# Means of the two directly multiplied tiles by two halving adds each, idle products gathered around them, and the opening's order dealt anew

## Chip, core and metric

One core of one Trainium2 chip. The metric is the device time of one execution in microseconds; 413.33 us is the median of three runs before the change (413.1 to 413.67).

## What is computed

Input x is 2048 tokens of 512 numbers. Cut to what matters:

```
x  = A_x                                   # 1 x 2048 x 512
xn = layernorm(x)
s  = attention(xn, wqkv) @ wo              # 32 heads of 16, each position looks at 8 positions, 2 apart
g  = silu(gelu(layernorm(xn) @ w1 + b1) @ w2 + b2)   # hidden width 1376
return x + s * g
```

The two layer norms each take a mean over the 512 numbers of a token and subtract it.

## The kernel before

Tokens are split by parity into two classes (an attention window of step 2 never leaves its class), each of 8 tiles of 128 tokens. The attention goes by units of one class and one block of eight heads (8 units, u = 0 to 7). A unit's q, k and v come from `qkv` (products at L864: per tile three groups of four products, the high half of x by the high half of wqkv, low by high, high by low, since numbers are kept as a high and a low fp16 half). VectorE does the attention itself (L930, L933, L988 ...). The hidden layer (L1143, L1186), interleaved with it on TensorE, and the output products (L1056, L1088) fill the rest of the program.

The change lies in the opening, before the first tile of unit 0. There:

- SyncE's queue loads, in this kernel's words: `t` 6 and 7 (in_A_xt_dram, 256 KB each: tiles 6 and 7 of class 0 already transposed, into U), `x` 0 to 7 (in_A_x_dram, 256 KB each, into prod), `q` 0 and 2 (the two halves of wqkv block 0, 384 KB each, into prod), `q` 4 and 6 (the halves of block 1, into U), and pieces of w1 and b1 (in_B_w_dram, in_B_b_dram).
- Tiles 6 and 7 are "direct": `center` sums the four 128-row blocks of the transposed tile to one (tile 6: a VectorE reduction at L685, then one fp32 product with a matrix of 1/512 at L691; tile 7: four fp32 products at L682) and VectorE subtracts the mean that these leave in PSUM (L693). `direct` then multiplies the centred fp32 tile by the unscaled fp32 wqkv block (L700: four products a tile). The trace has two records for one fp32 product of L682, L691 and L700.
- The other tiles: statistics on VectorE (L659, L660), factors (L714 to L731), scaling by ScalarE (L742, L744), VectorE (L751) or GpSimd (L748), then either four transposing products (L766) with high and low halves written by ScalarE (L770) and VectorE (L772, L773), or a transposing DMA (L756 to L758).
- The scale of a wqkv block comes from its squares: ScalarE squares each half with a running sum (L597), two small products with the matrix `fours` add over the partitions (L513), five VectorE instructions make a power of two (L524 to L542), and then ScalarE writes the high halves (L619) and VectorE (L626) or GpSimd (L553, L554) the low ones.
- `WAKE` idle products (L1305, `fours` by a 256-column bf16 operand, into a PSUM bank that nothing reads) can stand anywhere on TensorE's queue; 24 of them do, some between the others' work up to 56 us.

Every step is an operation with a number, counted as it is added to the plan, and the table `ORDER` (L73) lists all 1269 numbers in the order in which they are issued; an engine runs its own in that order and waits for what an operation reads. `MEANBY` says for each direct tile who sums.

Of the kernel before, what the change touches and what calls it, by code (L numbers as in the profile page):

```python
# [13 lines left out]
ALU = mybir.AluOpType  # L14
# [53 lines left out]
MEANBY = ('dve', 'pe', 'pool', 'pool')  # L68
# [299 lines left out]
PU1 = 0.969  # L368
PWARM = 0.9
PEV = 0.2698  # L370

PTOT = 0.5899

WAKE = 24
PS1 = 1.1561

QHI = 4

PQLO = 0.5225

# [19 lines left out]
def tile_mixer(ctx, tc, a_x, a_xt, a_wqkv, a_wo, b_w1, b_b1, b_w2, out):  # L400
    nc = tc.nc
    pl = Plan()
# [270 lines left out]
    def center(i):  # L673
        n = FP.index(i)
# [852 lines left out]
```

## Time and profile before

| | us |
|---|---|
| median of three runs | 413.33 (413.1 to 413.67) |
| the profiled execution | 412.45 |
| its span, first to last instruction | 410.6 |
| TensorE busy | 403.6 (98%), granted clock 1.000 |
| VectorE busy | 381.7 (93%) |
| ScalarE busy | 225.3 (55%) |
| GpSimd busy | 132.8 (32%) |

The profiled execution is 1.85 us longer than its span. Chain and timeline rows begin with the start and the duration in us from the span's first instruction; `L` numbers are lines of the program before; where the time is in square brackets it is idle time of the engine before the row, with what ended it. The records overlap on TensorE (a product's record lasts longer than the distance to the next), so the chain's rows, which do not overlap, are used for sums.

### The profile page before, as it was taken

What the parts mean: (1) busy time and instruction counts of PE and PEld (TensorE: products, weight loads), DVE (VectorE), ACT (ScalarE), POOL (GpSimd) and SP (SyncE); (2) the same over time, 40 slices, a digit from 0 to 9 for tenths busy, and PEclk for the clock granted to TensorE, in tenths of its full rate; (3) what the DMA queues carried; (4) which work ended last, traced back from release to release, by engine and by line L of the source; (5) the groups of instructions that cost most, each with busy time, mean ns of one, the idle gap of its engine ahead of it and who ended that gap; (6) DMA issues with size and microseconds to landing.
All of it is one profiled execution on the core that took longest, in us unless ns stands there. A gap on an engine that the chain in (4) does not pass through costs nothing.

```text
span 410.6 us, 5500 instructions
## 1 busy us (share of the span) xinstructions
PE 403.6 (98%) x2035; PEld 199.3 (49%) x2035; DVE 381.7 (93%) x386; ACT 225.3 (55%) x372; POOL 132.8 (32%) x141
## 2 busy tenths in 40 slices
PE   7999999999999999999999999999999999999996
PEld 4665544444444455445544554444445544444443
DVE  4999999999999999999889999899999989989985
ACT  4899987983989736633564164114523177236310
POOL 3833000053552434243423344233322505250012
PEclk9999999999999999999999999999999999999999
DMA  8947437240018372911251008610244462004874
GB/s 300 388 105 233 165 110 199 89 180 26 1 30 197 77 130 79 165 32 27 51 145 23 0 2 215 208 51 25 104 120 122 107 137 59 0 1 117 271 209 180
DMA packets 52627, 48.04 MB, mean 117 GB/s; under 512 B 37066, under 2 KB 37510, under 8 KB 52088
## 3 DMA queue, kind: packets, MB, share of 16 engines
q1 hardware_dynamic: 52600, 47.69, 41.8%
q8 instruction: 16, 0.26, 0.3%
q14 instruction: 11, 0.09, 0.1%
HBM read 24.40 MB, written 7.34 MB: 77 GB/s over the span
## 4 chain that ended last, share of the span: by engine, by line
PE 97%; DVE 1%; DMA 1%; ACT 0%; issue 0%; ACTq 0%; DVEq 0%
PE ps L864 30%; PE ps L1143 25%; PE z L1186 25%; PE ps L1056 5%; PE z L1088 2%; PE ps L1088 2%; PE z L1174 2%; PE pl L864 1%; PE pl L700 1%; DMA U<-in_A_xt_dram 1%; PE pl L1088 1%; PE z L700 1%; PE z L1177 1%; PE z L766 1%; PE z L1305 0%; DVE U L1120 0%
## 5 line engine op out<-in xcount | busy, mean ns | idle before, releaser
L864 PE MATMUL ps<-wq,yT 128*128 128x384 f16 (+1 forms) x708 | 129.3, 337 | 0.1
L1186 PE MATMUL z<-w,h 128*128 128x512 f16 x480 | 111.4, 379 | 0.0
L1143 PE MATMUL ps<-yT,w 128*128 128x512 f16 x480 | 109.1, 379 | 0.0
L864 PEld LDWEIGHTS <-yT 128*128 128x128 f16 x744 | 72.3, 98 | 58.5 <-issue 1.1
L930 DVE TENSOR_TENSOR prod<-U 128x2048 f32<-128x2048 f32 x32 | 73.8, 2312 | 4.1 <-ACT U L882 3.0
L1143 PEld LDWEIGHTS <-w 128*128 128x128 f16 x480 | 46.7, 98 | 55.6 <-issue 0.5
L933 DVE TENSOR_REDUCE L<-prod 128x128 f32<-128x2048 f32 x32 | 73.0, 2282 | 0.5
L1186 PEld LDWEIGHTS <-h 128*128 128x128 f16 x480 | 46.5, 98 | 54.6 <-issue 0.7
L999 POOL TENSOR_TENSOR prod<-prod,prod 128x1024 f32<-128x1024 f32 x14 | 41.3, 2970 | 81.4 <-DVE prod L988 81.4
L882 ACT ACTIVATE U<-ps,cs 128x384 f32<-128x384 f32 x54 | 30.2, 577 | 62.9 <-PE ps L864 62.7
L988 DVE TENSOR_TENSOR prod<-pl,U 128x2048 f32<-128x2048 f32 x28 | 63.5, 2283 | 0.3
L1156 ACT ACTIVATE ps<-ps,b1T,hsc 128x512 f32<-128x512 f32 x40 | 29.9, 748 | 37.2 <-PE ps L1143 37.0
L1159 ACT ACTIVATE h<-ps,hsc 128x512 f16<-128x512 f32 x40 | 27.4, 685 | 20.5 <-PE z L1186 19.5
L1009 POOL COPY gate<-prod 1x1 f32<-1x1 f32 x21 | 4.6, 221 | 102.2 <-DVE prod L930 102.2
L1010 POOL TENSOR_TENSOR prod<-prod 128x1024 f32<-128x1024 f32 x14 | 32.8, 2346 | 0.0
L1161 DVE SCALAR_TENSOR_TENSOR h<-ps,hsc,h 128x512 f16<-128x512 f32 x40 | 29.5, 744 | 3.3 <-ACT h L1159 3.3
L1056 PE MATMUL ps<-wo,oT 128*128 128x512 f16 x96 | 21.5, 379 | 0.0
L983 DVE TENSOR_TENSOR prod<-prod,prod 128x2048 f32<-128x2048 f32 x9 | 20.6, 2288 | 0.2
L971 ACT ACTIVATE o<-prod,osc 128x1024 f16<-128x1024 f32 (+1 forms) x9 | 9.5, 1052 | 18.1 <-DVE prod L983 9.9
L1010 POOL TENSOR_TENSOR prod<-prod,prod 128x1024 f32<-128x1024 f32 x7 | 16.4, 2347 | 0.0
L1088 PEld LDWEIGHTS <-oT 128*128 128x128 f16 x108 | 10.5, 98 | 10.4 <-issue 0.2
L1056 PEld LDWEIGHTS <-oT 128*128 128x128 f16 x96 | 9.4, 98 | 11.1
(201 smaller groups left out, 397.2 us busy)
## 6 DMA issues: line engine op xcount, KB each, us to landing
f<-in_A_x_dram SPq DMA_DIRECT2D x31, 256.0 KB, 3.1
U<-U SPq DMA_DIRECT2D x16, 392.0 KB, 6.2
gd<-f SPq DMA_DIRECT2D x12, 256.0 KB, 4.3
prod<-in_A_x_dram SPq DMA_DIRECT2D x8, 256.0 KB, 6.2
oT<-in_B_w_dram SPq DMA_DIRECT2D x2, 1024.0 KB
yT<-in_B_w_dram SPq DMA_DIRECT2D x2, 1024.0 KB
f<-gd SPq DMA_DIRECT2D x8, 256.0 KB, 5.0
out_dram<-f SPq DMA_DIRECT2D x8, 256.0 KB
```

The source lines that it names most:

```text
L864: nc.tensor.matmul(b.t[:, 0:wide], y[:, s, k, o:o + P], wq[hb][:, t, k], start=(n == 0), stop=(n == 11))
L882: act(384, lambda i=i, b=b: nc.scalar.activation(U3[:, i:i + 31:15, :], b.t[:, 0:384].rearrange("p (t e) -> p t e", t=3), AF.Identity, sca ...
L930: dve(2048, lambda p2=p2, g=g: nc.vector.tensor_tensor(p2(), q, slots(Ut, KH, 2 * g), op=ALU.mult), qk + [("kh", ub, 0), ("kh", ub, 1), (" ...
L933: dve(2048, lambda pr=pr, g=g: nc.vector.tensor_reduce(L3()[:, 2 * g:2 * g + 2], pr.t.rearrange("p (r f d) -> p r f d", r=2, d=DH), AX.X, ...
L988: dve(2048, lambda: nc.vector.tensor_tensor(pr.t.rearrange("p (r f d) -> p r f d", r=2, d=DH), A3()[:, 2 * g:2 * g + 2].rearrange("p r (f ...
L999: pool(2.4, lambda n=n: nc.gpsimd.tensor_tensor(acc.t[:, n:n + 1024], acc.t[:, n:n + 1024], p1.t[:, n:n + 1024], op=ALU.add), [acc, p1], [ ...
L1010: nc.gpsimd.tensor_tensor(x.t[:, 0:1024], x.t[:, 0:1024], y(), op=ALU.add)
L1056: nc.tensor.matmul(b.t, oT[:, hb, i // 4, s, i % 4], wo[:, t, hb], start=(hb == 0 and n == 0), stop=(hb == last and n == 2))
L1088: nc.tensor.matmul(b.t[:, cols], oT[:, hb, i // 4, s, i % 4], wo[:, t, hb, cols], start=(start and hb == 0 and n == 0), stop=(stop and hb ...
L1143: nc.tensor.matmul(b.t[0:M], w1[:, s, f * 512 + k * M:f * 512 + (k + 1) * M], yT[ch][:, t, k], start=(n == 0), stop=(n == 11))
L1156: act(512, lambda: nc.scalar.activation(b.t[0:M], b.t[0:M], AF.Gelu_apprx_tanh, bias=b1T[0:M, f:f + 1], scale=hsc[0:M, 1:2]), [b, ("b1T",) ...
L1186: nc.tensor.matmul(z.t, hl[s][:, t * P:(t + 1) * P], w2[:, w, f], start=(f == 0 and n == 0), stop=False)
```

## The change

- `MEANBY` becomes `halves` for both direct tiles: VectorE adds the upper two 128-row blocks to the lower two (128x256) and then the halves of the result (128x128), and one fp32 product follows, for tile 6 and tile 7 alike.
- `WAKE` goes from 24 to 23 idle products.
- `ORDER` is a new permutation, from the first entry to the last. Since tile 7 has one operation more and there is one idle product less, the total stays 1269.

```
-MEANBY = ('dve', 'pe', 'pool', 'pool')
+MEANBY = ('halves', 'halves', 'pool', 'pool')
...
-    0, 1, 240, 19, 2, 3, 4, 5, 6, 7, 8, 9, 10, 11, 133, 129, 113, 120, 112, 115, 130, 20, 21, 32, 33, 168, 114,
...
+    3, 0, 6, 4, 1, 2, 5, 7, 55, 19, 26, 33, 34, 111, 112, 113, 114, 115, 116, 117, 118, 119, 120, 121, 122, 123,
+    124, 125, 126, 127, 128, 20, 129, 27, 38, 28, 21, 168, 130, 131, 132, 133, 35, 36, 39, 8, 10, 9, 15, 11, 16,
...
-WAKE = 24
+WAKE = 23
...
         elif MEANBY[n] == "dve":
             dve(512, lambda: nc.vector.tensor_reduce(f3()[:, 0], x3.rearrange("p k t -> p t k"), AX.X, ALU.add),
                 [("xt", i)], [f], port=False, c=0.45)
+        elif MEANBY[n] == "halves":
+            with pl.fuse():
+                dve(256, lambda: nc.vector.tensor_tensor(f3(), x3[:, 0:2], x3[:, 2:4], op=ALU.add), [("xt", i)], [f])
+                dve(128, lambda: nc.vector.tensor_tensor(f3()[:, 0], f3()[:, 0], f3()[:, 1], op=ALU.add), [f], [f])
```

Lines behind L686 move down by four in the changed program (L691 becomes L695, L700 L704, L766 L770, L1305 L1309 and so on).

SyncE's queue, the first loads before (the operands name the tensors; in_A_xt is `t`, in_A_x `x`, in_A_wqkv `q`):

```order
L1258 DMA U_94<-in_A_xt_dram 128x512
L588 DMA prod_100<-in_A_wqkv_dram 128x768 x2
L1233 DMA prod_101<-in_A_x_dram 128x512 x2
L588 DMA U_94<-in_A_wqkv_dram 128x768
L1258 DMA U_94<-in_A_xt_dram 128x512
```

and in the changed program:

```order
L1237 DMA prod_100<-in_A_x_dram 128x512
L1262 DMA U_94<-in_A_xt_dram 128x512 x2
L1237 DMA prod_100<-in_A_x_dram 128x512
L588 DMA prod_101<-in_A_wqkv_dram 128x768 x2
L588 DMA U_94<-in_A_wqkv_dram 128x768
```

The halves of wqkv block 0 move from the second and third place behind both transposed tiles and two x tiles (tiles 2 and 0), to the fifth and sixth; tile 7's transposed load moves from the seventh place to the third. The sixth load before and the seventh in the changed program is the first half of block 1.

TensorE's queue from the mean of tile 6 to the first transposition before (`first` holds the matrix of 1/512 and the identity, `pl` and z_148 the direct tiles 6 and 7, s_126 the sums of squares of wqkv block 0 and s_127 those of block 1):

```order
L691 MATMUL ps_143<-f_103,first 128x128
L1305 MATMUL z_147<-first,fours 128x256
L700 MATMUL pl_146<-prod_100,U_94 128x384 x2
L513 MATMUL z_147<-s_126,fours 128x1
L700 MATMUL pl_146<-prod_100,U_94 128x384
L682 MATMUL ps_144<-U_94,first 128x128 x4
L700 MATMUL pl_146<-prod_100,U_94 128x384
L513 MATMUL ps_145<-s_127,fours 128x1
L766 MATMUL z_150<-first,prod_101 128x128 x4
```

and from there to the same place in the changed program (s_125 block 0, s_126 block 1):

```order
L695 MATMUL ps_143<-f_103,first 128x128
L1309 MATMUL z_147<-first,fours 128x256
L695 MATMUL ps_144<-f_104,first 128x128
L513 MATMUL z_147<-s_125,fours 128x1
L704 MATMUL pl_146<-prod_101,U_94 128x384 x3
L704 MATMUL z_148<-prod_101,U_94 128x384
L770 MATMUL z_150<-first,prod_100 128x128 x4
L513 MATMUL ps_145<-s_126,fours 128x1
L704 MATMUL pl_146<-prod_101,U_94 128x384
```

Weight loads and rows that only repeat are left out in both. Before, 7 idle products stand ahead of the mean of tile 6, 3 behind it, 1 behind the first two direct products, and 13 later. In the changed program 18 stand ahead of it, 1 between the two means, 4 behind the second, and none later; both sums of block 0 stand ahead of the first direct product, and the four products of L682 are gone.

ScalarE's queue from the high halves of block 0 on, before (L597 squares the second half of block 1, L742 and L744 scale an x tile):

```order
L619 ACTIVATE wq_82<-prod_100,qsc 128x384 x4
L770 CAST yT_89<-z_150 128x4x128
L597 ACTIVATE wq_83,s_127<-U_94 128x768
L742 ACTIVATE rb_155<-pb_154,rb_155 128x1
L744 ACTIVATE prod_101<-prod_101,rb_155 128x512
L770 CAST yT_89<-z_150 128x4x128
```

and in the changed program:

```order
L619 ACTIVATE wq_82<-prod_101,qsc 128x384 x4
L774 CAST yT_89<-z_150 128x4x128
L746 ACTIVATE rb_155<-pb_154,rb_155 128x1
L748 ACTIVATE prod_100<-prod_100,rb_155 128x512
L597 ACTIVATE wq_83,s_126<-U_94 128x768
L504 ACTIVATE wq_84,s_129<-h_113 128x4x96
L774 CAST yT_89<-z_147 128x4x128
```

The square of block 1's second half has moved behind the scaling of a tile. From there on the order of all engines differs in many places, with the same operations of the same sizes.

121 rows, old and new, of the table ORDER are left out of this document.

## The prediction

> **What bounds the kernel now.** I read the page's busy times and the head of its chain first, then the chain in order of time, since it shows where the opening ends and the steady flow begins.
>
> ```profile
> PE 403.6 (98%) x2035; PEld 199.3 (49%) x2035; DVE 381.7 (93%) x386; ACT 225.3 (55%) x372; POOL 132.8 (32%) x141
> ...
> PE 97%; DVE 1%; DMA 1%; ACT 0%; issue 0%; ACTq 0%; DVEq 0%
> ```
>
> TensorE is 97% of the chain that ends last, and VectorE is busy 93% of the span. So a microsecond counts where TensorE has no work, works slowly or does work that can be left out, and a lead of TensorE holds only if VectorE, nearly full as well, leads with it. The chain's opening rows:
>
> ```profile
> 0.74 2.70 DMA U<-in_A_xt_dram
> 3.44 0.02 issue
> 3.46 1.03 DVE f L685
> 4.49 0.04 issue
> 4.54 0.81 PE ps L691 x2
> 5.35 0.02 issue
> 5.37 0.70 DVE U L693
> 6.07 0.04 issue
> 6.11 2.93 PE pl L700 x4
> 9.04 0.21 PE z L1305
> 9.25 0.03 PE z L513 x2
> 9.29 0.78 PE pl L700 x2
> 10.06 0.89 PE ps L682 x8
> ...
> 12.06 0.44 PE z L766 x4
> 12.50 2.58 PE z L700 x8
> ...
> 15.89 0.65 PE ps L864 x4
> ...
> 27.64 1.95 PE pl L864 x12
> 29.59 0.01 PE z L518
> 29.59 1.32 PE ps L864 x8
> ...
> 40.83 0.11 PE z L1305
> ```
>
> Three things are to be seen. Up to 6.11 the chain is a load, a mean and a subtraction. The first four records of L700 take 2.93 / 4 = 0.73 us each, the eight at 12.50 2.58 / 8 = 0.32: at first TensorE runs at half rate, although the page shows a granted clock of 1.000. The row at 9.29 (two records in 0.78) has the turn. Against 0.32 each, the four cost 2.93 - 1.29 = 1.64 us. From about 24 us on the rows follow each other almost without gaps (27.64 to 29.59).
>
> **Where the loads land.** From the timeline I take who waited for a load, and when SyncE issues again: from the ninth load on an issue starts just as the load eight places before has landed (9.18 for tile 7's transposed load, 9.86 for the x tile behind it).
>
> ```profile
> 1.19 1.65 PE L1305 MATMUL z<-first,fours 128*128 128x256 bf16 x7 [1.19 <-DVE first L440]
> 4.50 0.84 ACT L597 ACTIVATE wq<-prod 128x768 bf16<-128x768 f32 x1 [2.49 <-DMA prod<-in_A_wqkv_dram]
> 5.55 0.84 ACT L597 ACTIVATE wq<-prod 128x768 bf16<-128x768 f32 x1
> 6.30 0.19 ACT L597 ACTIVATION_READ_ACCUMULATOR wq<-prod 128x1 f32 x1
> 6.35 0.69 DVE L659 BATCH_NORM_STATS2 bn<-prod 128x6 f32<-128x512 f32 x1 [0.29 <-DMA prod<-in_A_x_dram]
> 7.55 0.69 DVE L659 BATCH_NORM_STATS2 bn<-prod 128x6 f32<-128x512 f32 x1 [0.29 <-DMA prod<-in_A_x_dram]
> 8.50 0.84 ACT L597 ACTIVATE wq<-U 128x768 bf16<-128x768 f32 x1 [2.02 <-DMA U<-in_A_wqkv_dram]
> 9.18 0.33 SPq L1233 DMA_DIRECT2D prod<-in_A_x_dram  x1
> 9.86 0.33 SPq L1260 DMA_DIRECT2D h<-in_B_w_dram  x1
> ```
>
> Adding sizes in the order of issue, 256 KB are in by 3.46, 640 by 4.50, 1024 by 5.55, 1280 by 6.35, 1536 by 7.55, 1920 by 8.50, 2176 by 9.18 and 2432 by 9.86. I take it that the changed order lands the same bytes at the same times. Then an x tile is in by 3.46, the transposed tile 6 (512 KB) by 4.1, tile 7 (768) by 4.8, the next x tile (1024) by 5.55, the halves of wqkv block 0 (1408, 1792) by about 6.95 and 8.2 instead of 4.50 and 5.55; block 1's first half (2176) by 9.18 instead of 8.50, and the next x tile (2432) by 9.86, as before.
>
> **The change, part by part.** The halving adds (L689, L690) have no row of their own. The nearest are the same addition at other widths, at the end of the program and with the mean subtracted:
>
> ```profile
> 406.35 0.69 DVE L1127 TENSOR_TENSOR U<-U,f 128x512 f32<-128x512 f32 x1
> 407.47 0.42 DVE L1127 TENSOR_TENSOR U<-U 128x256 f32<-128x256 f32 x1
> ```
>
> 256 columns less save 0.27, so 128x256 costs 0.42 and 128x128 about 0.28 (bounds: 0 and 0.42): 0.7 a tile against 1.03 for the reduction, 0.4 more for VectorE over both tiles. They are hidden: statistics of the first x tile 3.46 to 4.3, halves of tile 6 to 5.0, of tile 7 to 5.7, statistics of the next x tile to 6.5, two subtractions of 0.70 to 7.9, all ahead of 9.2, which comes next.
>
> The direct products now stand behind both sums of block 0. The second half is in at 8.2, its square with the sum's read-out takes 6.49 - 5.55 = 0.94, so the sums reach TensorE at about 9.2. That is the time of the row at 9.25 before: in this profile the products of L513 waited there for the slow L700. So the block's scale, and all that follows from it, comes no later. But before, half of tile 6's eight records was done by then; now none is. In return tile 7's mean is done already, as one product instead of four, and all idle products as well (18 of 0.21 from 1.19 end at 5.0, where the mean of tile 6 follows; the rest ends at about 7).
>
> TensorE's account from 9.25 on, by the rows above: +4 records of L700, 1.29; -8 records of L682, -0.89; -10 idle products up to 24 us and -3 later (40.83 and two more), 13 x 0.11 = -1.42. Sum -1.02. The idle products before partly filled waits, so their removal is worth nothing where a wait stays. To see whether it does I followed the queues by hand, each engine in its new order with these rows:
>
> ```profile
> 9.99 2.13 ACT L619 ACTIVATE wq<-prod,qsc 128x384 f16<-128x384 f32 x4 [0.56 <-DVE qsc L542]
> ...
> 12.53 0.59 ACT L770 CAST yT<-z 128x512 f16<-128x512 f32 x1 [0.40 <-PE z L766]
> ...
> 13.91 0.29 ACT L742 ACTIVATE rb<-pb,rb 128x1 f32<-128x1 f32 x1
> ...
> 14.24 0.81 ACT L744 ACTIVATE prod<-prod,rb 128x512 f32<-128x512 f32 x1
> ```
>
> ScalarE's square of block 1's first half ends at 9.18 + 0.84 + 0.19 = 10.2, so the four high halves (L619) run from 10.2 to 12.4, 0.2 late, and the cast ends at 13.0. VectorE's scale takes 9.4 to 9.95, then three statistics of 0.82, the small L714 and L716 and one low half of 0.6 bring it to 13.1, which releases L742 and L744 (13.91 to 15.05: 1.14) until 14.3; only then comes the square of block 1's second half, until 15.3 with its sum. On TensorE, eight records of tile 6 and six of tile 7 (14 x 0.32 = 4.5) and two transpositions (0.88) last from 9.28 to 14.7, and there its L513 waits for that square: **a new wait of 0.7 us** (none in the best case, 1.5 if VectorE or GpSimd is late by 0.8). Behind it the groups of L864 find their operands: by my walk TensorE has done 16 records of L700 (5.16), four transpositions (1.76), 19 groups of four L864 (19 x 0.65 = 12.35) at 9.28 + 19.3 + 0.8 = 29.4. Before, at 29.59, 18 groups were done (ending with the chain's row at 27.64). Lead: 0.65 + 0.19 = **0.84 us**. The three late idle products add 0.33, for the row at 40.83 is followed without a gap.
>
> VectorE gains as well: with less idle time in the opening, it reaches w1's scale (L522) at 29.1 by the same walk, where before
>
> ```profile
> 30.33 0.15 DVE L522 TENSOR_REDUCE s<-z 128x1 f32<-128x4 f32 x1
> ...
> 380.00:398.00 18.00, 18.00 (x89) 8.26 (x88) 17.00 (x14) 5.26 (x7) 1.06 (x1) 1.00 0.84 246
> 398.00:411.00 13.00, 8.77 (x49) 4.50 (x46) 7.51 (x13) 0.00 (x0) 3.11 (x3) 1.00 0.53 178
> ```
>
> stood at 30.33: 1.2 us ahead. The two rows by stretch (busy us of TensorE, weight loads, VectorE, ScalarE, GpSimd) show why that matters: VectorE works 17 of the 18 us before the last output products, so without its lead they would not start earlier. Elsewhere the re-dealt order changes no total. Two places that I find tight (a result of block 0 read back late on ScalarE, at 30 and at 33 us) cost 0.4.
>
> Sum on the profiled execution: 412.45 - 0.84 - 0.33 + 0.4 = 411.7. The median is 0.88 above that execution. I know no row that explains it; one candidate is that full rate came later in those runs, since each microsecond of it costs half a microsecond. The changed program's idle products come long before its real ones, so it would lose less to that. I take half of the 0.88: **412.1 us**.
>
> [...] The row at 1.19 shows seven idle products of 0.21 (half rate), and after the 2 us pause up to 4.54 half rate again until after 9.25. [...]
>
> **The rivals.**
>
> Half rate is back at 9.25 (slower). By the same rows, as a mechanism of this kernel: TensorE is empty from 7 to 9.2, before it was empty for 2.0 us at 2.5 and ran at half rate afterwards. If the pause ends full rate, the direct products run at 0.64 instead of 0.32 for as long as before (6.11 to 9.3, 3.2 us), and 1.6 us are lost: 411.7 + 1.6 = 413.3 against 412.45, and 0.85 above the median is 414.2. [...] For it: half rate after the earlier pause; against it: that pause followed only 1.5 us of work, this one 6.
>
> The lead is given back. TensorE leads, but VectorE, ScalarE or a transposing load comes later somewhere in the re-dealt order, so waits return: at most the whole 0.84 and 0.33, with the new 0.4: about 413.2 beside the median (412.6 to 414.2). For it: VectorE's 93%; against: its own 1.2 us.
>
> The loads come quicker. If each half of wqkv costs only what it cost before (1.05 us from 4.50 to 5.55) behind the x tile at 5.55, the second is in at 7.65 and the sums at 8.6: 0.5 more, 411.6.
>
> **How the numbers follow.** Forecast 0.45 (412.1, own range 411.5 to 412.7); lead given back 0.24; half rate 0.18; quicker loads 0.13. The range 411.2 to 414.3 leaves out the far ends of the second and third. A measurement of this kernel can tell about 0.2%, or 0.83 us. Faster than 412.50: most of the forecast (0.36), the quicker loads (0.12), a little of the second (0.02), 0.5. Slower than 414.16: half rate mostly (0.13) and the second's end (0.07), 0.2. The rest, 0.3, lies between.
>
> **What would show it.** In the changed profile: the first L704 at 9.2 (8.6 for quicker loads; later than 9.7 and the landing rule is wrong), its records 0.32 apart (0.64 for half rate), an L513 waiting about 0.7 us near 15, 19 groups of four done near 29.4, no idle product behind 7 us, L522 near 29.1. The prediction is wrong if TensorE's idle time behind 35 us grows by more than a microsecond, or if VectorE's lead is gone by 100 us.

## The result and the profile after

The changed kernel takes **414.11 us** (median of 20 runs, 412.14 to 415.10), the kernel before on the same chip 413.16 (20 runs, 412.48 to 413.86): ratio 1.0022, 95% interval 1.0015 to 1.0029. It is a little slower, where the forecast was 412.1. The time of the rival "half rate is back" was 414.2.

The profiled execution took 415.04, with a span of 413.2, so it lies near the upper end of the runs; a second trace (414.34, span 412.6) is among the experiments. The busy times and the head of the chain say as little as those of before:

```profile
PE 405.0 (98%) x2028; PEld 200.4 (48%) x2028; DVE 383.7 (93%) x389; ACT 229.9 (56%) x376; POOL 135.4 (33%) x141
...
PEclk9799999999999999999999999999999999999999
```

The second row, the granted clock (full speed is 1) in 40 slices, does: in the second slice (10 to 20 us) it is a 7. The stretches give it in figures (us; busy time of TensorE, weight loads, VectorE, ScalarE, GpSimd; granted clock; DMA share; GB/s):

```profile
10.00:20.00 10.00, 9.89 (x33) 5.91 (x33) 6.51 (x24) 6.56 (x16) 5.13 (x5) 0.70 1.04 410
```

and for the kernel before:

```profile
10.00:20.00 10.00, 9.95 (x60) 6.26 (x59) 9.13 (x28) 8.78 (x17) 8.29 (x9) 1.00 1.03 405
```

TensorE is as busy as before but gets through 33 records instead of 60, at a clock of 0.70; VectorE, which waits for it, falls from 9.1 to 6.5 busy microseconds. TensorE's timeline shows where:

```profile
5.11 0.79 PE L695 MATMUL ps<-f,first 128*128 128x128 f32 x2
5.70 0.34 PE L1309 MATMUL z<-first,fours 128*128 128x256 bf16 x1
7.25 0.49 PE L695 MATMUL ps<-f,first 128*128 128x128 f32 x2 [1.21 <-DVE f L690]
7.58 0.60 PE L1309 MATMUL z<-first,fours 128*128 128x256 bf16 x4
9.09 0.16 PE L513 MATMUL z<-s,fours 128*128 128x1 bf16 x1 [0.91 <-ACT wq L597]
10.05 0.16 PE L513 MATMUL z<-s,fours 128*128 128x1 bf16 x1 [0.81 <-ACT wq L597]
10.15 4.18 PE L704 MATMUL pl<-prod,U 128*128 128x384 f32 x6
14.12 1.49 PE L704 MATMUL z<-prod,U 128*128 128x384 f32 x2
15.40 0.93 PE L770 MATMUL z<-first,prod 128*128 128x128 f32 x4
```

The four idle products at 7.58 are issued 0.109 us apart: the rate is full by then. Then TensorE is empty for 0.91 and 0.81 us with only one sum of 128x1 between, and the eight records of L704 from 10.15 to 15.40 take 5.25 us (0.77 for the first, seven times 0.64): the rate is half again. The transpositions at 15.40 still go at 0.21; at about 16.0 the spacing returns to 0.32 a record. The granted clock, read over short stretches, tells when (the last figure but two of a row):

```profile
5.84:9.24 3.40, 1.28 (x9) 0.80 (x8) 2.73 (x7) 1.11 (x3) 0.00 (x0) 1.00 0.99 371
9.25:12.65 3.40, 2.60 (x5) 1.51 (x5) 2.22 (x10) 3.35 (x8) 2.64 (x2) 0.50 1.05 398
12.66:16.06 3.40, 3.40 (x9) 1.90 (x8) 2.79 (x8) 0.36 (x1) 1.01 (x2) 0.50 1.05 416
16.08:19.48 3.40, 3.35 (x19) 2.16 (x18) 1.02 (x4) 3.07 (x8) 2.03 (x3) 1.00 1.04 419
```

It went to half at 9.24 us, as TensorE ran empty behind the first sum, and back to full at 16.07, 6.83 us later. The trace's list of clock changes begins with the change to full at 5.83. The stretch from there to 9.24 is 3.41 us long, and TensorE was busy for 1.28 us of it; twice the same length follows at half rate. The section on the hardware comes back to this. The chain of waits has the same delay (start, us):

```profile
3.07 5.97 DMA prod<-in_A_wqkv_dram
...
9.07 0.94 ACT wq L597 x2
...
10.05 0.16 PE z L513
10.22 4.11 PE pl L704 x6
...
31.73 0.01 PE z L518
```

The sum that stood at 29.59 before (L518) stands at 31.73.

For comparing traces I use one figure, the **lost time** up to a moment: the moment minus the work that TensorE had begun by then, each record taken at the shortest spacing its shape shows (0.109 us for 128 columns in fp32, 0.322 for 384; 0.162, 0.202 and 0.216 for 384, 480 and 512 in fp16; 0.03 for a small sum), idle products at nothing. The whole work so counted is 395.76 us before and 395.10 after (eight records less, two more).

| lost by (us) | 9 | 12 | 18 | 40 | 400 |
|---|---|---|---|---|---|
| before | 7.49 | 8.15 | 9.05 | 9.82 | 10.85 |
| before, second trace | 7.49 | 8.28 | 9.26 | 10.14 | 11.06 |
| after | 8.56 | 10.55 | 12.75 | 13.50 | 13.99 |
| after, second trace | 8.56 | 10.55 | 12.10 | 12.85 | 13.34 |
| both pauses filled | 8.56 | 9.26 | 10.02 | 10.47 | 10.96 |
| two products woven in | 7.92 | 8.15 | 10.35 | 10.80 | 11.18 |
| one product woven in | 7.92 | 8.15 | 9.70 | 10.15 | 10.64 |

Before to after: 3.14 lost more by 400 us, 0.66 less work, so 2.5 us; the spans differ by 2.6. This execution lies near the upper end of its runs and the one of before (412.45) below all 20 of its own, so the medians differ by less, 0.95. The loss is all made by 18 us (3.70); from 40 to 400 us the changed order loses less than before (0.49 against 1.03).

### The profile page after: what moved, and what is told of

Same layout as the page of the kernel before. It is cut to its first block, busy times and chain, and to the rows that moved or that the text cites. A ratio compares the mean times of both kernels' runs of the same rounds, so it can differ in the third digit from the quotient of the medians.

```text
span 413.2 us, 5511 instructions
## 1 busy us (share of the span) xinstructions
PE 405.0 (98%) x2028; PEld 200.4 (48%) x2028; DVE 383.7 (93%) x389; ACT 229.9 (56%) x376; POOL 135.4 (33%) x141
## 4 chain that ended last, share of the span: by engine, by line
PE 95%; DMA 1%; ACT 1%; DVE 1%; issue 1%; SPq 1%; DVEq 0%; ACTq 0%
PE ps L868 30%; PE ps L1147 25%; PE z L1190 25%; PE ps L1060 5%; PE z L1092 2%; PE ps L1092 2%; PE z L1178 2%; DMA prod<-in_A_wqkv_dram 1%; PE pl L868 1%; PE pl L704 1%; PE pl L1092 1%; PE z L1181 1%; PE z L704 0%; PE z L770 0%; ACT wq L597 0%
## 5 line engine op out<-in xcount | busy, mean ns | idle before, releaser
L868 PE MATMUL ps<-wq,yT 128*128 128x384 f16 (+1 forms) x708 | 128.4, 337 | 0.0
L1190 PE MATMUL z<-w,h 128*128 128x512 f16 x480 | 112.7, 379 | 0.0
L1147 PE MATMUL ps<-yT,w 128*128 128x512 f16 x480 | 110.3, 379 | 0.0
L868 PEld LDWEIGHTS <-yT 128*128 128x128 f16 x744 | 72.7, 98 | 58.9 <-issue 0.8
L934 DVE TENSOR_TENSOR prod<-U 128x2048 f32<-128x2048 f32 x32 | 74.8, 2340 | 2.4 <-ACT U L886 1.2
L1003 POOL TENSOR_TENSOR prod<-prod,prod 128x1024 f32<-128x1024 f32 x14 | 39.6, 2850 | 64.1 <-DVE prod L992 64.0
L1014 POOL TENSOR_TENSOR prod<-prod,prod 128x1024 f32<-128x1024 f32 x7 | 16.4, 2347 | 0.0
L1092 PEld LDWEIGHTS <-oT 128*128 128x128 f16 x108 | 10.5, 98 | 10.4 <-issue 0.2
```

Of the source, the lines that this page charges most:

```text
L868: nc.tensor.matmul(b.t[:, 0:wide], y[:, s, k, o:o + P], wq[hb][:, t, k], start=(n == 0), stop=(n == 11))
L934: dve(2048, lambda p2=p2, g=g: nc.vector.tensor_tensor(p2(), q, slots(Ut, KH, 2 * g), op=ALU.mult), qk + [("kh", ub, 0), ("kh", ub, 1), (" ...
L1003: pool(2.4, lambda n=n: nc.gpsimd.tensor_tensor(acc.t[:, n:n + 1024], acc.t[:, n:n + 1024], p1.t[:, n:n + 1024], op=ALU.add), [acc, p1], [ ...
L1014: nc.gpsimd.tensor_tensor(x.t[:, 0:1024], x.t[:, 0:1024], y(), op=ALU.add)
L1092: nc.tensor.matmul(b.t[:, cols], oT[:, hb, i // 4, s, i % 4], wo[:, t, hb, cols], start=(start and hb == 0 and n == 0), stop=(stop and hb ...
L1147: nc.tensor.matmul(b.t[0:M], w1[:, s, f * 512 + k * M:f * 512 + (k + 1) * M], yT[ch][:, t, k], start=(n == 0), stop=(n == 11))
```

## The experiments

Theory A: TensorE's pause ahead of the direct products brings half rate back, and this is what the change cost. Rival B: the cost is the later landing of wqkv. In the diffs, numbers in the order are operations; those of added idle products are 134 and up, and each later number rises by their count, which the diffs leave out. The count of idle products (`WAKE`, 23) rises or falls with them. In four kernels a line of the program has a lower number than in after: by 3 with one or both pauses filled, by 4 with the direct products first, by 5 without the first idle products. Four direct products of a tile are eight records.

**Both pauses filled**, and **the second filled**:

```diff
-    20, 129, 27, 38, 28, 21, 168, 130, 131, 132, 133, 35, 36,
+    20, 129, 134..139, 27, 38, 28, 21, 168, 130, 131, 132, 133, 140..157, 35, 36,
```

```diff
-    130, 131, 132, 133, 35, 36,
+    130, 131, 132, 133, 134..151, 35, 36,
```

> The changed kernel with 24 more idle products (L1309): 6 behind the one that follows the mean product of tile 6, 18 behind the four that follow the mean product of tile 7, so that TensorE is not empty from 5.9 to 7.25 us nor from 8.0 to 10.05 us. Nothing else moves. Theory A (the half rate of the direct products, 0.64 us a record from 10.15 to 15.4 us and again on to 16.0 us, is a consequence of these pauses and is what the change cost): the first direct product starts at about 10.2 us and its records stand 0.32 apart; the first eight end 2.5 us earlier, and the time falls by 1.5 to 3 us to 411.0 to 412.6. Rival B (the later landing of the halves of wqkv, 9.04 us instead of 6 us, sets the time, through VectorE and ScalarE; the rate of the direct products is hidden): records 0.32 apart, but the time stays at 413.7 to 414.5. If the records stay 0.64 apart, the pauses are not what took the rate away.

> The changed kernel with 18 more idle products behind the four that follow the mean product of tile 7 only: the pause 8.0 to 10.05 us is filled, the one from 5.9 to 7.25 us stays. Theory A1 (what counts is whether TensorE stood idle just ahead of the direct products): as with both pauses filled, records 0.32 apart, 411.0 to 412.6. Theory A2 (what counts is a stretch of some 3.4 us that has to be busy all through, whose ends in the trace of after lie near 5.85, 9.25, 12.65 and 16.05 us, where the rate changes): the stretch 5.85 to 9.25 has 1.35 us of pause, so the rate may be lost at 9.25 and come back at 12.65 us: about half of the gain, 412.3 to 413.3. Rival B: 413.7 to 414.5 whatever the rate.

Measured: 412.86 (412.45 to 413.30; before 413.04; ratio 0.9996, 0.9987 to 1.0005) and 412.94 (411.54 to 413.71; 0.9990, 0.9977 to 1.0003). TensorE with both filled:

```profile
6.92 2.56 PE L1306 MATMUL z<-first,fours 128*128 128x256 bf16 x22
9.32 0.17 PE L510 MATMUL z<-s,fours 128*128 128x1 bf16 x1
9.64 0.16 PE L510 MATMUL z<-s,fours 128*128 128x1 bf16 x1 [0.16 <-ACT wq L594]
9.74 2.17 PE L701 MATMUL pl<-prod,U 128*128 128x384 f32 x6
11.76 0.81 PE L701 MATMUL z<-prod,U 128*128 128x384 f32 x2
12.40 0.60 PE L767 MATMUL z<-first,prod 128*128 128x128 f32 x4
```

The eight records take 12.40 - 9.74 = 2.66 us instead of 5.25. With work that does nothing, 1.1 us of time came back (1.0022 to 0.9996 of before), and the whole loss against before. The order of the loads was not touched, so **theory A holds** for the sign: the pauses are what made the change slower. The size falls a little short of what A expected (411.0 to 412.6): not all that the direct products gain reaches the end. One place where it stops is the end itself. There the chain with both pauses filled has

```profile
396.52 4.50 DMA oT<-o
...
401.07 4.40 PE z L1089 x21
```

TensorE is ahead and waits 0.31 us for the transposing load of the last attention output.

What the first pause does alone is not shown: in the trace with the second filled, tile 7 landed at 5.17 us and its mean product started at 6.00, so there was no first pause. Its second sum still waited 0.78 us, and the clock stayed full.

**Without the first 18 idle products:**

```diff
-WAKE = 23
+WAKE = 5
```

> The changed kernel without the 18 idle products that open TensorE's work (1.19 to 5.0 us); the 5 around the mean products stay. Theory A: since the rate was lost again before the direct products began, these 18 bought nothing in the changed kernel: the direct products stand 0.64 apart as in after until about 16 us, and the time is that of after, 413.7 to 414.6. Rival D (the idle products still pay, the rate of the direct products depends on what ran before 5 us): the half rate lasts longer, 1 to 2 us more, 415 to 416.

Measured: 414.42 (412.82 to 415.34; 1.0032, 1.0018 to 1.0046): that of after within the intervals, as A said. The direct products are at 0.64 either way:

```profile
9.93 4.18 PE L699 MATMUL pl<-prod,U 128*128 128x384 f32 x6
13.89 1.49 PE L699 MATMUL z<-prod,U 128*128 128x384 f32 x2
```

**The direct products of tile 6 ahead of the sums:**

```diff
-    131, 132, 133, 35, 36, 39,
+    131, 132, 133, 22, 23, 24, 25, 35, 36, 39,
```

> The changed kernel with the four direct products of tile 6 ahead of the two L513 sums on TensorE instead of behind them. They need the first half of wqkv, which landed at 8.07 us, and the second, 9.04 us, not the sums of squares, which were ready at 10.05 us. Theory A: the pause shrinks from 2.05 us to a few tenths twice, the direct products start at about 8.1 us instead of 10.15 and stand 0.32 apart; the four end at about 9.75 us, those of tile 7 near 11.2 us instead of 15.4; the time falls to 410.5 to 412.3. If the rate is still lost (the pause from 5.9 to 7.25 us stays), the start alone gives up to 2 us of TensorE's time: 412 to 413.3. Rival B: the direct products are not on the path, 413.7 to 414.5, or later still because the sums wait for the products.

Measured: 415.43 (414.37 to 417.94; 1.0069, 1.0045 to 1.0094), slower than all of the expectations but rival B's last words. The rate stays full at the direct products, yet:

```profile
8.71 2.85 PE L700 MATMUL pl<-prod,U 128*128 128x384 f32 x8 [1.23 <-DVE pb L714]
11.39 0.19 PE L509 MATMUL z<-s,fours 128*128 128x1 bf16 x2
...
16.22 0.66 PE L766 MATMUL z<-first,prod 128*128 128x128 f32 x4 [2.69 <-DVE prod L751]
```

The sums come 1.3 us later than in after, the scale of wqkv and all of VectorE's queue behind it with them, TensorE waits 2.69 us at 16.22, and from 18.1 to 21.3 us its records are at half rate once more. So the sums are on the path as well: a chain sums, scale, statistics, normalised tiles, transpositions runs beside TensorE's own work. In this trace the second half of wqkv landed at 9.53 us, the latest of all.

**Loads of wqkv first**, and **loads and sums first**:

```diff
-    3, 0, 6, 4, 1, 2, 5, 7, 55, 19, 26, 33, 34,
+    0, 1, 2, 6, 3, 4, 5, 7, 19, 26, 55, 33, 34,
...
-    20, 129, 27, 38, 28, 21, 168, 130, 131, 132, 133, 35, 36,
+    20, 129, 134..147, 27, 38, 28, 21, 168, 130, 131, 132, 133, 148..151, 35, 36,
```

```diff
-    3, 0, 6, 4, 1, 2, 5, 7, 55, 19, 26, 33, 34,
+    0, 1, 2, 6, 3, 4, 5, 7, 19,
...
-    20, 129, 27, 38, 28, 21, 168, 130, 131, 132, 133, 35, 36,
+    20, 21, 26, 33, 34, 129, 130, 131, 132, 133, 134..137, 35, 22, 36, 37, 48, 46, 44, 23, 27, 28, 24, 25, 55, 38, 168,
```

> The changed kernel with the loads issued in the order transposed tile 6, both halves of wqkv's first block, transposed tile 7, x tiles 2 and 0, and then as before; VectorE's statistics of x tile 2 stand behind the sums of both transposed tiles; 18 more idle products (14 behind the one after the mean product of tile 6, 4 behind those after tile 7's), so that the rate is not lost. Theory A with the rest of the explanation (once the rate is kept, the later landing of wqkv's second half and with it the sums of its squares, 9.64 us where both pauses were filled, is what stands between that kernel and the forecast): the second half lands 1.5 to 3 us earlier, the sums come at 7.5 to 8.3 us, and the time falls by another 0.7 to 1.5 us to 411.2 to 412.2. Rival (VectorE's chain of statistics and the x tiles, now 2 us later, set the end of the opening): 412.6 to 413.4, as with the pauses filled alone.

> The changed kernel with the loads as in the kernel with the loads reordered, 4 more idle products behind those around the mean products, and TensorE's order: mean product of tile 6, 9 idle products, first sum, first direct product, second sum, second direct product, mean product of tile 7, the other two direct products; VectorE's and ScalarE's parts of this (subtraction, scale, the three parts of the split) stand in the same order, the statistics of x tiles 2 and 0 behind them. Theory A with the landing: the sums come at 5.6 and 6.6 us instead of 9.6 to 10, the direct products of tile 6 end at 9.0 to 9.5 us instead of 12.3 to 12.7, the clock stays full from 6 us on, and the opening ends 2 to 3 us earlier than with the pauses filled: 410.0 to 411.5. Rival (the later tiles x, which land no earlier than in the changed kernel, set the end of the opening through VectorE's statistics): 412.3 to 413.3.

Measured: 413.46 (412.82 to 414.80; before 413.12; 1.0009, 0.9998 to 1.0020) and 415.40 (414.77 to 415.64; 1.0050, 1.0038 to 1.0063). Both forecasts of theory A fail: the sums come at 8.5 us, or the first at 6.55 and the second at 7.80, well ahead of after, and the time does not follow. Nor do they speak for rival B; but what the earlier landing is worth can't be read from these two kernels, for in both TensorE then waits for something else. In the first, VectorE's statistics of two x tiles stand ahead of its subtractions:

```profile
8.50 0.19 PE L513 MATMUL z<-s,fours 128*128 128x1 bf16 x2
10.58 3.90 PE L704 MATMUL pl<-prod,U 128*128 128x384 f32 x6 [1.89 <-DVE pb L718]
14.28 0.84 PE L704 MATMUL z<-prod,U 128*128 128x384 f32 x2
```

TensorE waits 1.89 us, and the rate is half from 10.93 to 14.34 us: theory A's loss once more, from another wait. But this profiled execution (414.80, mean granted clock 0.996) is the slowest of its 12 runs, and one other is like it; the other ten had 0.999 to 1.000 and a median of 413.38. So most runs kept the rate and were still no faster than before. That is what the expectation's rival forecast, with VectorE's statistics and the x tiles in the way; its range ended at 413.4. In the second, all direct products up to 10.9 us run at full rate, and then the x tiles, whose loads now come last, are missing:

```profile
10.06 0.81 PE L704 MATMUL z<-prod,U 128*128 128x384 f32 x2
14.42 0.66 PE L770 MATMUL z<-first,prod 128*128 128x128 f32 x4 [3.55 <-POOL prod L752]
```

a wait of 3.55 us for the first normalised tile, and half rate from 15.97 to 19.39 us. All five runs of this kernel had a granted clock of 0.990 to 0.995.

**The means alone**, on the kernel before:

```diff
-MEANBY = ('dve', 'pe', 'pool', 'pool')
+MEANBY = ('halves', 'halves', 'pool', 'pool')
...
+        elif MEANBY[n] == "halves":
...
```

with its order as it was, tile 7's two additions behind the scale on VectorE, its mean product behind the fourth direct product of tile 6.

> The kernel before with one part of the change alone: the means of both transposed tiles are summed by halves on VectorE; its order of loads and operations stays, but that tile 7's two additions stand behind the scale of wqkv's block 0 on VectorE and its mean product behind the fourth direct product of tile 6; 24 idle products as before. TensorE has 0.66 us less to do (two L695 records of 0.22 us in all for eight L682 records of 0.89 us). Theory A (the means were no part of the loss; it came from the order of the opening): 0.3 to 0.7 us below the kernel before, ratio 0.9983 to 0.9993. Rival (VectorE, which adds about 0.7 us for tile 7 between the scale and the splits, gives it back): 0 to 0.5 us above, ratio 1.000 to 1.0012.

Measured: 413.11 (412.45 to 413.53; 0.9997, 0.9988 to 1.0006): neither gain nor loss, between the two. Its trace shows a wait of 1.30 us in front of the mean product of tile 7, for the additions which now stand late on VectorE:

```profile
8.29 1.54 PE L704 MATMUL pl<-prod,U 128*128 128x384 f32 x4
11.13 0.49 PE L695 MATMUL ps<-f,first 128*128 128x128 f32 x2 [1.30 <-DVE f L690]
```

So 0.66 us less work on TensorE is not yet time: it has to meet a place where TensorE does not wait. What the means would give elsewhere is left open.

**Two direct products woven in**, and **one**:

```diff
-    20, 129, 27, 38, 28, 21, 168, 130, 131, 132, 133, 35, 36,
+    20, 129, 134..139, 27, 38, 28, 21, 168, 130, 131, 132, 133, 22, 23, 35, 36,
```

```diff
-    132, 133, 22, 23, 35, 36,
+    132, 133, 22, 35, 36, 23,
```

> The changed kernel with 6 more idle products behind the one after the mean product of tile 6, and with the first two direct products of tile 6, which need only the first half of wqkv (8.07 us), ahead of the two L513 sums on TensorE; the other two stay behind them. So the pause of 8.0 to 10.05 us is filled with work of the kernel instead of idle products. Theory A: the rate is kept (records 0.32 apart), 1.29 us of direct products move into time that was empty, the sums stay at 9.5 to 10.1 us: 411.3 to 412.4. Rival (what follows the sums on ScalarE and VectorE sets the end of the opening, so that TensorE's room before it is worth nothing): as with the pauses filled, 412.6 to 413.3.

> The kernel in which the first two direct products of tile 6 stand ahead of the two L513 sums, with one of them moved back: TensorE takes one direct product, both sums, then the next three. There the second sum waited for the second direct product (9.82 us, though ScalarE had the square of the second half at 9.2), and VectorE stood idle from 8.4 to 10.1 us for the scale behind it. Theory C (once the rate is kept, the chain sums, scale, statistics, first transposes sets the end of the opening): the second sum at about 9.2 to 9.5 us, the continuous stretch of L868 0.3 to 0.6 us earlier, the time 411.8 to 412.3. Rival (what the opening gives is no longer worth anything, since the end of the program, the transposing DMA of the last attention output at 401 us, is as late): 412.3 to 412.8, as with the two products first.

Measured: 412.43 (411.74 to 412.99; 0.9982, 0.9973 to 0.9990) and **412.05** (411.48 to 413.05; before 413.17; 0.9976, 0.9965 to 0.9987). Both are faster than the kernel before and after. The second's rows:

```profile
8.46 0.91 PE L704 MATMUL pl<-prod,U 128*128 128x384 f32 x2 [0.94 <-DVE pb L718]
9.21 0.19 PE L513 MATMUL z<-s,fours 128*128 128x1 bf16 x2
9.26 1.54 PE L704 MATMUL pl<-prod,U 128*128 128x384 f32 x4
```

Its sums are at 9.21 instead of 9.82, the lost time by 18 us is 0.65 less, and its span 409.8 instead of 410.4. This fits theory C: once the rate is kept, the sums and what follows them set the end of the opening. The medians differ by 0.38, but each stands beside its own runs of before and their intervals overlap, so the step between the two is shown by the traces rather than by the times.

**Second traces, and eight idle products:** the two kernels unchanged, and after with 0.9 us of the second pause filled.

```diff
-    130, 131, 132, 133, 35, 36,
+    130, 131, 132, 133, 134..141, 35, 36,
```

> The changed kernel unchanged, for a second trace, since its profiled execution (415.04) lay near the upper end of its runs (412.14 to 415.10). Theory A: its pause between the last idle product and the sums is again about 2 us and the direct products stand 0.64 apart; with a second half of wqkv at 8.2 to 8.9 us instead of 9.04, 413.3 to 414.6. If the records stand 0.32 apart in this one, the loss of the rate is a matter of the single execution, and the time is 412 to 413.

> The kernel before unchanged, for a second trace. If loads land as they did in the first (both halves of wqkv at 4.48 and 5.53 us, the eighth load at 9.84), first direct product at about 6.1 us, full rate from about 9.4 us on, 412.5 to 413.3. If the sixteen DMA engines drift apart here too (some of them 1 us late, as in the trace of after), the eighth load lands at 10.3 to 11 us, and the time is 413.3 to 414.

> The changed kernel with 8 instead of 18 more idle products behind the four that follow the mean product of tile 7: about 0.9 us of the pause of 2 us is filled, 1.1 us stays. Theory A with a bound (in the traces so far every pause of up to 1.8 us left the rate full, every one of 2.05 us and more took it): records 0.32 apart, 412.5 to 413.3, as with 18. Theory A2 (the whole stretch of about 3.4 us has to be busy): the rate is lost as in after, 413.7 to 414.5.

Measured: after again 414.34. Its tile 7 landed at 5.27 us instead of 6.42, so its mean product comes earlier and the pause is only longer; the rate is half again:

```profile
6.43 0.60 PE L1309 MATMUL z<-first,fours 128*128 128x256 bf16 x4
9.10 0.16 PE L513 MATMUL z<-s,fours 128*128 128x1 bf16 x1 [2.07 <-ACT wq L597]
10.07 0.16 PE L513 MATMUL z<-s,fours 128*128 128x1 bf16 x1 [0.81 <-ACT wq L597]
10.17 4.18 PE L704 MATMUL pl<-prod,U 128*128 128x384 f32 x6
```

Before again took 413.28, with the eighth load at 9.91 (9.84 in the first trace). Eight idle products: 412.60 (411.15 to 414.73; 0.9987, 0.9970 to 1.0004), the widest spread of all. Its trace keeps the rate,

```profile
8.24 0.16 PE L513 MATMUL z<-s,fours 128*128 128x1 bf16 x1 [0.28 <-ACT wq L597]
9.21 0.16 PE L513 MATMUL z<-s,fours 128*128 128x1 bf16 x1 [0.81 <-ACT wq L597]
9.31 2.17 PE L704 MATMUL pl<-prod,U 128*128 128x384 f32 x6
```

but two of its 12 runs had a granted clock of 0.994 and 0.996 and took 414.43 and 414.73; the other ten 0.998 to 1.000, and 411.15 to 413.46. So eight are nearly enough, and it varies from run to run whether the rate is lost; with 18 or with woven products no run was below 0.998.

The 20 runs of after sort in the same way, with no edit between them:

| mean granted clock | runs | median (us) |
|---|---|---|
| 0.989 to 0.992 | 12 | 414.34 |
| 0.994 to 0.996 | 6 | 413.45 |
| 1.000 | 2 (412.14 and 413.69) | |

Over 412 us, 0.996 answers to 3.3 us at half rate. The trace at 0.990 has the 6.83 us seen above and 1.2 us behind its last products, where they cost nothing. A second stretch of 3.41 us goes with 0.9 us more, so in the unchanged kernel, too, the time goes with the rate.

## Why the prediction was wrong

**The step that failed** is the rate: the sum rests on records of L704 0.32 us apart from 9.28 on, right behind a pause of 2.2 us (7 to 9.2). That such a pause leaves the rate full was my assumption; no run before the change shows it, and in the changed kernel the eight records took 5.25 us, 0.64 apart. The rival had the mechanism, its place and its sign; I gave it 0.18, because the earlier pause in the trace of before had followed 1.5 us of work and this one would follow six. That earlier pause could show nothing of it: in the trace of before the clock is first granted in full at 9.20 us, so there was no full rate to lose. In the changed kernel the longest gap ahead of the loss was 1.21 us: in the 3.40 us up to 9.24 TensorE was busy for 1.28 us, in three pieces, and the rate was gone, whatever had gone before (18 idle products without a gap). The rival's price, 1.6 us, rested on half rate "for as long as before", 3.2 us. In the trace the clock was half for 6.83 us, of which the products felt 5.9 (10.15 to about 16.0), and by 15 us the lost time was 11.93 us, with both pauses filled 9.42: 2.5 us, of which 0.4 is the sums' (10.05 against 9.64). By the ratios to before, 1.0022 and 0.9996, filling the pauses is worth 1.1 us of the time.

That the rival's 414.2 is so near to the 414.11 is luck. It added 1.6 us for the rate to a gain of 0.75 (412.45 to 411.7). Measured were 1.1 us for the rate and, with both pauses filled, a gain of 0.2 (0.9996 of before).

**The landing rule, "the same bytes at the same times", failed** by the test that the prediction named: the first L704 came at 10.15, not 9.2. When SyncE issues again shows it, as before, by the load eight places ahead:

```profile
7.10 0.33 SPq L1264 DMA_DIRECT2D h<-in_B_w_dram  x1
8.09 0.33 SPq L588 DMA_DIRECT2D U<-in_A_wqkv_dram  x1
9.06 0.33 SPq L1237 DMA_DIRECT2D prod<-in_A_x_dram  x1
10.04 0.33 SPq L1264 DMA_DIRECT2D oT<-in_B_w_dram  x1
```

The halves of wqkv were in at 8.07 and 9.04 instead of 6.95 and 8.2, block 1's first half at 10.03 instead of 9.18. The rule took one trace for all: with the load order of after, nine traces have the second half at 8.03 to 9.53 us, and the forecast was the early end of that. It made the pause 0.85 us longer and the sums as much later.

**The lead of 0.84 us at 29.4** hangs on the landing too, even with the rate kept. With both pauses filled TensorE has begun 18.25 groups of L868 by then, with one product woven in 18.75, after itself 13.75; the forecast was 19, and before had 18. VectorE's scale of w1 (L522) comes at 32.79 in after, 29.71 with the pauses filled and 29.35 with one product woven in, against 30.33 before and 29.1 forecast. What is missing with the pauses filled is mostly the later sums, 9.64 against 9.2, and then VectorE's chain behind them. Where both conditions of the walk held, it came out: in the trace with eight idle products the second half of wqkv was in at 8.20 (8.2 forecast), the second sum started at 9.21, the rate was kept, 19.0 groups had begun by 29.4, L522 stood at 29.29, and this execution took 411.54, where the sum for the profiled one was 411.7. That is one execution, near the fast end of its runs (411.15 to 414.73).

**Right were the smaller terms.** The halving adds took 0.41 and 0.29 (0.42 and 0.28 forecast):

```profile
L689 DVE TENSOR_TENSOR f<-U x2: 392/408/424, 4.3 to 6.4; 128x256 f32<-128x256 f32 x2
```

```profile
L690 DVE TENSOR_TENSOR f<-f x2: 291/292/292, 4.8 to 6.9; 128x128 f32<-128x128 f32 x2
```

(ns: shortest, median, longest). The new wait near 15 us is there once the rate is kept: with both pauses filled, spacings between 13.9 and 16.0 us exceed the shortest by 0.16, 0.26 and 0.19, 0.61 together, where 0.7 was forecast; in after it is hidden by TensorE's own lateness. Of the two tight places one cost 0.23 us in after (at 33.85); the other, 0.15 at 36.63, stands in the trace of before as well (34.83), so 0.4 was too much. The re-dealt order changes no total for the worse: 0.49 us lost from 40 to 400 us against 1.03 and 0.92 in the two traces of before, and 0.33 of the difference is the three late idle products, as forecast. This half microsecond and the 0.66 of work are what the change gains on TensorE. That a lead of TensorE holds only with what VectorE feeds it showed at 401 us, where TensorE waited for the last attention output.

**The half of 0.88** added for the median rested on a later full rate in the other runs. The second trace of before has it 0.6 us later (granted in full from 9.81, against 9.20) and lost 0.21 more by 18 us; that explains little of the 0.8 by which its span is longer. Another 0.3 is a wait for the last attention output at 401.6 us. What the rest is stays open.

## What to carry to other kernels

The load order that gathered idle products and preparations ahead of the first long products opened a pause just in front of them. Here that pause was paid twice: as 0.91 and 0.81 us of waiting, and as 6.83 us of half rate behind it. So look at the spacing of the first records on both sides of a pause. Ask how much of each 3.4 us TensorE works, not how long the longest gap is; in the table below the rate was kept in every stretch with 2.01 us of work or more, and lost in every one with 1.63 us or less. Fill what is missing, best with work whose operands are already there, without pushing back the small operation on which another engine waits. A landing time taken from one trace is one draw: ask what the plan does if it is a microsecond later.

## What the runs showed of the hardware

- In five traces the granted clock changed only at times that lie a whole number of stretches of 3.41 us apart: 5.83, 9.24 and 16.07 us in after, 4.57, 7.98 and 14.81 in its second trace, 4.10, 10.93 and 14.34 with the loads of wqkv first, 4.34, 18.00 and 21.41 with the direct products first, 5.73, 15.97 and 19.39 with loads and sums first. Where the first one falls differs from execution to execution.
- The stretches of the table sort by what TensorE did in the whole stretch, and not by the longest pause in it. The groups overlap a little (1.72 us of work kept the rate, 1.89 lost it): the busy time counts the records, whose ends are modelled, so a limit near half of a stretch is an estimate from this table:

| stretch of 3.4 us at full rate (from, us) | TensorE busy in it, us | longest pauses, us | rate behind it |
|---|---|---|---|
| after (5.84) | 1.28 | 1.21, 0.91 | half |
| loads and sums first (12.57) | 1.41 | 3.55, in part | half |
| loads first (7.52) | 1.51 | 1.89 | half |
| directs first (14.59) | 1.63 | 2.69, in part | half |
| after again (4.58) | 1.89 | 2.07, in part | half |
| loads and sums first (9.15) | 1.72 | 3.55, in part | full |
| directs first (4.35) | 2.01 | 0.98 | full |
| two products woven in (11.41) | 2.19 | 1.20 | full |
| means alone (7.62) | 2.21 | 1.30, in part | full |
| eight idle products (6.59) | 2.32 | 0.28, 0.81 | full |

- So one and the same pause can cost the rate or not: with the loads first, two of 12 runs lost it (mean clock 0.996, the others 0.999 to 1.000); unchanged, two of the 20 runs of after kept it (1.000, the others 0.989 to 0.996). That the place of the stretches decides this is argued from the traces, for the other runs have a mean clock alone.
- In two traces the loss did not come with the pause. After 2.69 us (to 16.22) the records were still at 0.32 and went to half at 18.00, where a stretch ended; after 3.55 us (to 14.42) at 15.97.
- Half rate lasted one stretch (18.00 to 21.41, 15.97 to 19.39, 10.93 to 14.34) where work filled it, and two where the first of them was in part empty (after, both traces: busy 2.60 and 1.49 of 3.40 us). The stretches that took the rate away were not empty: they held 1.28 to 1.89 us of work, and the longest gap in front of the loss was 1.21 us in after, 1.89 us with the loads first.
- The granted clock did not show the half rate at the start of these kernels: 1.000 in the trace of before, with records of L700 0.64 apart, and 0.998 without the first idle products, with L704's 0.64 apart from 9.93 to 15.2 us. In all fourteen traces the list of clock changes begins with the first change to full (9.20 and 15.25 us in these two), and the figure reads 1.00 ahead of it. There the spacing of equal records is the surer sign.
- By the DMA engines' records, the sixteen engines do not finish a load together in each execution: the third load's last part came between 4.83 and 6.42 us in nine traces with one order of loads, and at 5.53, 5.85 and 7.26 us in three with the order of before, where, in the late ones, some engines ran 1 us or more behind the rest. Later loads inherited it.
